# Turning the rows of experts 2 to 7 on VectorE, by way of memory, in a fused attention and mixture-of-experts kernel

## The chip, the cores and the metric

The kernel runs on one core of a Trainium2 chip. A core has a matrix engine (TensorE, PE in the profile, with its weight loads shown apart as PEld), a vector engine (VectorE, DVE), a scalar engine (ScalarE, ACT), a general engine (GpSimd, POOL) and a synchronization engine (SyncE, SP) that here only issues transfers. Transfers run on 16 DMA engines and are issued from the instruction streams of SP and POOL. Each engine works through its own stream in order, and waits where an instruction's operands are not ready. The metric is device time in microseconds (us), the median of several runs.

## The reference: what is computed

Sliding-window attention over 8 batches, 8 heads and 576 positions (half of the heads with a dilated window), and after it a top-1 mixture of 8 experts over the 4608 tokens of 512 features:

```
x = attn_out.transpose(0, 2, 1, 3).reshape(B * S, H * D)      # 4608 x 512
logits = x @ w_gate;  expert_idx = argmax(logits);  gate_w = softmax(logits)[expert_idx]
for e in range(8):
    xe = x[expert_idx == e]
    out[expert_idx == e] = gate_w * (relu(xe @ w1[e]) @ w2[e])   # w1 512x1024, w2 1024x512
```

## The kernel before

**Attention and routing.** The attention stage writes its rows to `x_d` in memory. Routing puts into the table `pair`, for every expert, the token number and the gate of each of its slots, in blocks of 128.

**Experts.** Each expert has a `Static` job of four blocks of 128 rows (512 slots; expert 0 has two blocks and two more as `rest0`). What does not fit goes to `Dynamic` jobs, called overflow below: five big ones (`DBIG`) of 128 rows, and two small ones (`Tail`) of 32 rows. Which expert an overflow job belongs to is known only at run time; `blocks_info` looks that up (seven indirect reads into `look`), and finds the rows `ti` and the weight rows `wi`.

**Weights.** An expert has 8 units of 512 KB, four of `w1` and four of `w2`. A unit is loaded into one of three `raw` buffers and split into a high and a low fp32r part (`split_unit`: ScalarE copies, VectorE subtracts, two halves each). A load is asked for three units ahead. Static units are loaded by SP; overflow units by POOL, with an indirect transfer that takes its 128 row numbers from `wi`.

**Rows.** A block's rows are gathered by POOL (`gather`, an indirect transfer into one of four `xg` buffers). A matrix multiplication needs them with features on the partitions, so TensorE turns them, four 128x128 transposes against `ident` into one PSUM tile `tpx` (only one buffer), ScalarE copies the high part out and VectorE subtracts for the low part (`prep`, `prep_x`; lines 799, 802, 806 for static blocks, 900, 902, 903 for big overflow jobs, 995 and 1002 for tails).

**Order.** In the expert stage the streams of TensorE, VectorE and ScalarE are in the order in which the program is written (`manual_schedule`); those of POOL and SP are ordered by the scheduler. While expert i runs (8 pieces of its first layer `hps`, f = 0 to 7, 12 matrix multiplications each; then 4 blocks of its second layer `yps` in halves, k = 0 to 7, 12 each), the 8 units of an overflow job and the 8 of expert i+1 are split, that overflow job runs in two layers of 24 (`hpd`, `ypd`) with its own transposes `tph`, and expert i+1's rows are gathered and turned. Each finished block is scaled by ScalarE into `y` and written out by POOL (`finish`).

Of the kernel before, what the change touches and what calls it, by code (L numbers as in the profile page):

```python
# [25 lines left out]
NE = 8  # L26
# [24 lines left out]
TAIL = 32  # L51
DBLK = DBIG + DTAIL
# [71 lines left out]
def _layout(q, k, v, wg, w1, w2):  # L124
# [8 lines left out]
    def spans(a, step, width):  # L133
# [17 lines left out]
            w1.reshape(NE, 4, P, DF),  # L151
# [4 lines left out]
    w = np.ascontiguousarray(w).reshape(NE * 8 * P, DF)  # L156
# [4 lines left out]
def attention_moe_kernel(ctx, tc, qk, v, wg, w, cst, tok, end, slots, mask, zero, out):  # L161
# [594 lines left out]

    def finish(y_ps, gate, it_col):
        y = pools["y"].tile([P, DM], F32, name="y")
        nc.scalar.activation(y, y_ps, AF.Copy, scale=gate)  # L759
        nc.gpsimd.indirect_dma_start(  # L760
            out=out,
            out_offset=bass.IndirectOffsetOnAxis(ap=it_col, axis=0),
            in_=y,
            in_offset=None,
        )

    class Static:
        def __init__(self, e, rows=N, nblk=4):
# [5 lines left out]
            self.ahead = {}  # L774

# [12 lines left out]
        def fetch(self, i):  # L788
            self.xg[i] = gather(self.it[i], self.rows)
# [20 lines left out]
        def prep(self, i):  # L810
            self.turn_x(i)
            self.high_x(i)
            self.low_x(i)
# [5 lines left out]
        def load(self, u):  # L819
            raw = raws.tile([P, DF], F32, name="raw")  # L820
            r = (self.e * 8 + u) * P
            nc.sync.dma_start(raw, w[r : r + P])
# [61 lines left out]
    class Dynamic:  # L884
        def __init__(self, ti=None, wi=None, gate=None, fixed=None, units=None):
            self.ti, self.wi, self.gate, self.fixed = ti, wi, gate, fixed
            self.units = [] if units is None else units
            self.ahead = {}

        def fetch_x(self):  # L890
# [4 lines left out]
            self.xg = gather(self.it)  # L895

        def prep_x(self):
            tp = pse.tile([P, 4, P], F32, tag="E", name="tpx")
# [8 lines left out]
        def load(self, u):  # L907
            raw = raws.tile([P, DF], F32, name="raw")
            nc.gpsimd.indirect_dma_start(  # L909
                out=raw,  # L910
                out_offset=None,
                in_=w,
                in_offset=bass.IndirectOffsetOnAxis(ap=self.wi[:, u : u + 1], axis=0),
            )
            return raw

# [58 lines left out]
    class Tail(Dynamic):  # L975
# [3 lines left out]
        def __init__(self, ti, gate, parts, wi, tag):  # L979
            super().__init__(ti, wi, gate)  # L980
            self.own, self.parts, self.tag = ti, parts, tag

        def fetch_x(self):
            self.xg = gp.tile([P, DM], F32, name="xg")
            nc.gpsimd.indirect_dma_start(
                out=self.xg[:TAIL],
                out_offset=None,
                in_=x_d[:],
                in_offset=bass.IndirectOffsetOnAxis(ap=self.own, axis=0),
            )  # L990

        def prep_x(self):
            tp = pse.tile([P, 4, TAIL], F32, tag="E", name="tpx")
            for c in range(4):
                nc.tensor.transpose(
                    tp[:, c], self.xg[:TAIL, c * P : (c + 1) * P], ident[:TAIL, :TAIL]
                )
# [4 lines left out]
            nc.scalar.copy(self.x, tp)  # L1002

        def unit(self, to, u):
            if u % 2 == 0 and to in (0, 1, 2):
                self.pair = new_unit(to)
            if to in (0, 1, 2):
                to = self.pair[:, u % 2].bitcast(F32)
            nc.gpsimd.indirect_dma_start(
                out=to,  # L1010
                out_offset=None,
                in_=w,
                in_offset=bass.IndirectOffsetOnAxis(ap=self.wi[:, u : u + 1], axis=0),
            )
# [182 lines left out]
    def blocks_info(d, nd):  # L1197
# [30 lines left out]
        at_ = dsp.tile([P, nd], I32, name=f"at{nd}")  # L1228
        nc.vector.tensor_tensor(at_, sl, cc[:, C_AT - C_ATT : C_AT + nd - C_ATT], op=ALU.add)
        yield  # L1230
        look = dsp.tile([P, nd, 2], I32, name=f"look{nd}")
        for i in range(nd):
            nc.gpsimd.indirect_dma_start(
# [3 lines left out]
                in_offset=bass.IndirectOffsetOnAxis(ap=at_[:, i : i + 1], axis=0),  # L1237
            )
            yield
        shp = [P, nd, NE]  # L1240
        wi = dsp.tile(shp, I32, name=f"wi{nd}")
        nc.vector.tensor_tensor(
            wi,
            ew.broadcast_to(shp),
            cc[:, C_PU - C_ATT : C_PU + NE - C_ATT].unsqueeze(1).broadcast_to(shp),
            op=ALU.add,
        )
        yield
        no = dsp.tile([P, nd], F32, name=f"no{nd}")
# [4 lines left out]
        ti = dsp.tile([P, nd], I32, name=f"ti{nd}")  # L1254
        nc.vector.tensor_tensor(ti, look[:, :, 0], no, op=ALU.add)
        yield
        info["blocks"] = ti, wi, look[:, :, 1].bitcast(F32)
# [3 lines left out]
    def make_list():  # L1261
# [84 lines left out]
        yield from blocks_info(d_all, DBLK)  # L1346
        dti, dwi, dgt = info["blocks"]
        parts = dsp.tile([P, DTAIL], I32, name="parts")
        nc.vector.tensor_scalar(
# [3 lines left out]

        dyn[:] = [Dynamic(dti[:, i : i + 1], dwi[:, i], dgt[:, i : i + 1]) for i in range(DBIG)]
        dyn[DBIG:] = [
            Tail(
                dti[:TAIL, DBIG + i : DBIG + i + 1],
                dgt[:, DBIG + i : DBIG + i + 1],
                parts[:, i : i + 1],
                dwi[:, DBIG + i],  # L1360
                tag,
            )
            for i, tag in enumerate(("xd", "hs"))
        ]
# [8 lines left out]
    with tc.manual_schedule(engines=ENGS):  # L1373
# [13 lines left out]

        nx.begin()
        r0.fetch_x()
        nx.fetch(0)  # L1390
        r1.fetch_x()
# [3 lines left out]
        st_.layer2(0, range(6))  # L1395
        some_gates(1)
        st_.layer2(1, range(6))
        r0.prep_x()
        nx.fetch(2)
        some_gates(1)  # L1400
        st_.layer2(0, range(6, 8))
        r0.layer1([0])
        some_gates(1)
        nx.prep(0)
        nx.fetch(3)
        part(0)
        some_gates(1)
        r0.layer1([1])
        some_gates(1)
        r0.turn([0])  # L1410
        r1.prep_x()
        r0.turn([1])
# [189 lines left out]
```

## Time and profile before

| what | value |
|---|---|
| median of 3 runs | 639.79 us (639.29 to 640.07) |
| profiled execution, its own time | 634.56 us |
| its span, first to last instruction | 632.8 us |
| TensorE busy | 604.8 us (96%) |
| VectorE, ScalarE, POOL busy | 348.5, 314.2, 249.7 us |
| granted TensorE clock, mean | 0.984 |
| moved by DMA | 138.70 MB, mean 219 GB/s |

The profiled execution is 5.2 us shorter than the median of the runs; of its own time 1.8 us lie around the span. Attention and routing take about the first 190 us of the span, experts the rest. A row of a timeline merges like instructions that follow each other; its first number is its start, so that the start of the next row less its own start is what it took of the engine's stream. A row of windows gives the stretch and its length, then busy time and number of instructions of PE, PEld, DVE, ACT and POOL, the granted clock (1.00 is 2.4 GHz), the DMA share and GB/s.

### The profile page before, as it was taken

The numbers are of one execution on the slowest core, as the hardware profiler recorded it, in microseconds if no ns is written. First come the engines' busy times: TensorE is split into PE (matmuls) and PEld (weight loads), VectorE is DVE, ScalarE is ACT, GpSimd is POOL, SyncE is SP. The second block draws the span as 40 slices with busy tenths as digits, with TensorE's granted clock in tenths as the row PEclk, the third lists the DMA queues.
The fourth block names the chain that finished last, engine by engine and source line by source line (L and its number), as shares of the span: only waits on it lengthen the run. The fifth ranks groups of instructions, "written<-read, shape, count | busy, mean of one in ns | idle before, by whom it ended". The sixth has DMA issues, their size and how long they took to land. (4 is left out here: it accounts for less than half of the span.)

```text
span 632.8 us, 13319 instructions
## 1 busy us (share of the span) xinstructions
PE 604.8 (96%) x5299; PEld 492.2 (78%) x5299; DVE 348.5 (55%) x749; ACT 314.2 (50%) x606; POOL 249.7 (39%) x301
## 2 busy tenths in 40 slices
PE   7999999998889999899999999999999999999992
PEld 6877887776677888788888888888888888887771
DVE  3777888889584559325554455455454544552100
ACT  2667677687523645334653455456445544552200
POOL 0332465689835540642133224222421244242221
PEclk7999999999899999999999999999999999999997
DMA  8999999976226575453675376547735765865310
GB/s 332 409 398 412 400 405 409 340 238 204 67 87 232 155 234 198 122 178 120 197 232 184 116 236 221 172 137 231 236 128 181 239 199 161 307 223 218 133 55 21
DMA packets 43295, 138.70 MB, mean 219 GB/s; under 512 B 8880, under 2 KB 10288, under 8 KB 43184
## 3 DMA queue, kind: packets, MB, share of 16 engines
q1 hardware_dynamic: 23376, 78.99, 35.6%
q0 software_dynamic: 19856, 58.84, 27.6%
q8 instruction: 42, 0.69, 0.4%
q14 instruction: 21, 0.17, 0.1%
HBM read 118.18 MB, written 21.63 MB: 221 GB/s over the span
## 5 line engine op out<-in xcount | busy, mean ns | idle before, releaser
L724 DVE TENSOR_TENSOR wu<-raw,wu 128x512 fp32r<-128x512 f32 x200 | 127.9, 687 | 85.6 <-ACT wu L723 85.6
L874 PE MATMUL yps<-wu,h 128*128 128x512 f32 x696 | 171.4, 398 | 0.0
L843 PE MATMUL hps<-x,wu 128*128 128x512 f32 (+1 forms) x720 | 165.2, 386 | 0.2 <-DVE h L855 0.2
L843 PEld LDWEIGHTS hps<-x,wu 128*128 128x128 f32 x720 | 132.0, 188 | 28.1 <-DVE h L855 0.4
L874 PEld LDWEIGHTS yps<-wu,h 128*128 128x128 f32 x696 | 128.1, 188 | 27.8 <-issue 0.8
L723 ACT CAST wu<-raw 128x512 fp32r<-128x512 f32 x200 | 112.1, 619 | 2.4 <-DMA raw<-in_w_dram 2.4
L854 ACT ACTIVATE h<-hps 128x512 fp32r<-128x512 f32 (+1 forms) x60 | 35.0, 583 | 97.0 <-PE hps L843 87.9
L855 DVE SCALAR_TENSOR_TENSOR h<-hps,h 128x512 fp32r<-128x512 f32 (+1 forms) x60 | 40.3, 672 | 77.4 <-ACT h L854 77.4
L909 POOL DMA_INDIRECT raw<-in_w_dram,wi x40 | 38.1, 952 | 96.8 <-DVE wu L724 92.6
L327 ACT COPY pts<-pt 96x512 f32<-96x512 f32 x72 | 41.9, 582 | 49.6 <-PE pt L322 48.7
L760 POOL DMA_INDIRECT out_dram<-y,pair x30 | 31.5, 1051 | 67.4 <-ACT y L759 38.8
L759 ACT ACTIVATE y<-yps,pair 128x512 f32<-128x512 f32 x28 | 19.3, 688 | 74.4 <-PE yps L874 47.9
L301 DVE TENSOR_REDUCE nm<-s 128x4 f32<-128x384 f32 x72 | 39.5, 549 | 23.8 <-PE s L290 23.7
L322 PE MATMUL pt<-ident,p 128*96 128x128 f32 x288 | 48.2, 292 | 2.5 <-ACT pts L327 2.3
L369 POOL DMA_DIRECT2D x_d<-xs x36 | 20.5, 569 | 67.4 <-DVE xs L357 30.8
L337 PE MATMUL o<-vr,pts 96*64 96x65 f32 x1152 | 43.9, 229 | 2.3 <-issue 1.4
L337 PEld LDWEIGHTS o<-vr,pts 96*64 96x64 f32 x1152 | 38.5, 142 | 9.6 <-issue 7.8
L749 POOL DMA_INDIRECT xg<-x_d,pair x30 | 30.7, 1025 | 35.8 <-PE tpx L799 18.4
L306 DVE TENSOR_TENSOR d<-s,nm 128x384 f32<-128x384 f32 x72 | 40.0, 557 | 4.6
L316 ACT ACTIVATE p<-d 128x384 f32<-128x384 f32 x72 | 37.5, 524 | 7.5 <-DVE d L306 7.4
L964 PE MATMUL ypd<-wu,hd 128*128 128x512 f32 x168 | 40.5, 392 | 0.0
L932 PE MATMUL hpd<-wu,xd 128*128 128x512 f32 x168 | 40.4, 395 | 0.0
(172 smaller groups left out, 694.8 us busy)
## 6 DMA issues: line engine op xcount, KB each, us to landing
raw<-in_w_dram SPq DMA_DIRECT2D x65, 512.0 KB, 4.3
qkr<-in_qk_dram SPq DMA_DIRECT2D x36, 576.0 KB, 8.7
vr<-in_v_dram SPq DMA_DIRECT2D x36, 520.0 KB, 8.4
x_d<-xs POOLq DMA_DIRECT2D x44, 128.0 KB
t_in<-tab SPq DMA_DIRECT2D x3, 320.0 KB, 4.1
x_d<-xs POOLq DMA_DIRECT2D x8, 112.0 KB
x_d<-xs POOLq DMA_DIRECT2D x8, 96.0 KB
tab<-in_zero_dram SPq DMA_DIRECT2D x2, 320.0 KB, 8.2
```

What stands on the lines that cost most here:

```text
L301: nc.vector.tensor_reduce(st["nm", n][:, g], st["s", n][g], axis=AX.X, op=ALU.max)
L306: nc.vector.tensor_tensor(st["d", n][:, g], st["s", n][g], st["nm", n][:, g].broadcast_to([P, HP, KB]), op=ALU.subtract,)
L322: nc.tensor.transpose(pt[:KB, h], st["p", n][:, g, h], ident)
L327: nc.scalar.copy(st["pts", n][:, g], st.pop(("pt", n))[:KB])
L337: nc.tensor.matmul(st["o", n][QB * j : QB * (j + 1), g, h], lhsT=pts[:, g, h, QB * j : QB * (j + 1)], rhs=vr[:KB, n % NRV, a : a + DH + 1] ...
L723: nc.scalar.copy(u[:, 0, sl], raw[:, sl])
L724: nc.vector.tensor_tensor(u[:, 1, sl], raw[:, sl], u[:, 0, sl].bitcast(F32), op=ALU.subtract)
L843: nc.tensor.matmul(hps[:, : self.ns], lhsT=u[:, wpart, fs], rhs=self.x[:, xpart, c, : self.ns], start=(k == 0), stop=(k == 11),)
L855: nc.vector.scalar_tensor_tensor(h[:, 1, :n], hps[:, :n], 0.0, h[:, 0, :n].bitcast(F32), op0=ALU.max, op1=ALU.subtract,)
L874: nc.tensor.matmul(yps, lhsT=self.h[f][:, hpart, ts], rhs=u[:, wpart, fs], start=f == 0 and k == 0, stop=f == 7 and k == 2,)
L932: nc.tensor.matmul(hps, lhsT=self.x[:, xpart, c], rhs=u[:, wpart, ns], start=(k == 0), stop=(k == 11),)
L964: nc.tensor.matmul(self.yps, lhsT=self.h[f // 4][:, hpart, f % 4], rhs=u[:, wpart, fs], start=f == 0 and k == 0, stop=f == 7 and k == 2,)
```

## The change

It does five things.

1. For experts 2 to 7 and all overflow jobs, the transposes on TensorE go. POOL gathers a block one expert ahead (`collect`); SP writes it to a buffer `rows` in memory (`put`); about an expert later SP reads it back with four transfers of 32 partitions (`quarters`, pieces of 512 bytes), so that feature group i of all 128 rows stands on partitions 32i to 32i+31; VectorE transposes the 16 blocks of 32x32 in place with one instruction, ScalarE copies the high part and VectorE subtracts (`turned_split`). The rows of `w1` are permuted on the host to fit; experts 0 and 1 keep the transposes on TensorE and have an unpermuted copy of `w1`.
2. Tails gather 128 pieces of 128 features and are turned by one VectorE instruction on 128x128.
3. Overflow weights are loaded by SP at an address that SP reads from `wi` (`value_load`), not by POOL.
4. The streams of POOL and SP too are now in written order.
5. The list of overflow blocks (`make_list`) is computed earlier, partly beside the end of expert 0; the seven look-ups are issued one at a time; the last part of it, `no`, `ti` and `parts`, comes later. The gate scatters of expert 0's stage are issued earlier, and `r0.layer2` stands in other pieces.

```diff
+    def put(xg):
+        rows = dram.tile([P, DM], F32, name=f"rows{len(kept)}")
+        kept.append(rows)
+        nc.sync.dma_start(rows[:], xg)
+        return rows
+    def quarters(rows):
+        xg = gp.tile([P, DM], F32, name="xg")
+        parts = rows[:].rearrange("(s t) (i c) -> i t s c", s=NQ, i=NQ)
+        for i in range(NQ):
+            nc.sync.dma_start(
+                xg[i * QD : (i + 1) * QD].rearrange("t (s c) -> t s c", s=NQ), parts[i]
+            )
+        return xg
+    def turned(xg, n=NQ):
+        blocks = xg.rearrange("p (s c t) -> p s c t", s=n, c=4)
+        nc.vector.transpose(blocks, blocks)
+        return blocks.rearrange("p s c t -> p c s t")
+    def turned_split(x, xg):
+        rows = turned(xg)
+        x = x.rearrange("p i c (s t) -> p i c s t", s=NQ)
+        nc.scalar.copy(x[:, 0], rows)
+        nc.vector.tensor_tensor(x[:, 1], rows, x[:, 0].bitcast(F32), op=ALU.subtract)
...
         def load(self, u):
             raw = raws.tile([P, DF], F32, name="raw")
-            nc.gpsimd.indirect_dma_start(
...
+            self.bring(raw, u)
             return raw
+        def bring(self, to, u):
+            if self.at is None:
+                self.at = nc.sync.value_load(self.wi, min_val=0, max_val=(NE - 1) * 8 * P)
+            nc.sync.dma_start(to, w[bass.ds(self.at + u * P, P)])
...
-    with tc.manual_schedule(engines=ENGS):
+    with tc.manual_schedule(engines=ENGS | {mybir.EngineType.Pool, mybir.EngineType.SP}):
...
             st_, nx, dy = statics[i], statics[i + 1], dyn[i - 2]
-            nx.fetch_x()
+            nx.begin()
             for f in range(8):
+                if f == 0:
+                    dy.fetch_x()
+                elif f in (2, 3, 4, 5):
+                    nx.fetch(f - 2)
                 st_.layer1([f])
-                if f in (1, 3, 5, 6):
+                if f in (0, 2, 4, 5):
                     split()
-                if f == 4:
+                if f == 3:
                     dy.prep_x()
+                if f == 6:
+                    nx.prep(0)
             for k in range(2):
                 dy.layer1([k])
                 split()
+            nx.prep(1)
             for k in range(8):
                 st_.layer2(k // 2, halves[k % 2])
...
-                if k in (0, 2, 4, 6):
-                    nx.prep(k // 2)
-                if k == 4 and i < NE - 2:
-                    dyn[i - 1].fetch_x()
+                if k in (2, 4):
+                    nx.prep(k // 2 + 1)
+                if k % 2 == 0 and i < NE - 2:
+                    statics[i + 2].collect(k // 2)
+                if k % 2 and i < NE - 2:
+                    statics[i + 2].put(k // 2)
+                if k == 5 and i < NE - 2:
+                    dyn[i - 1].collect()
+                if k == 7 and i < NE - 2:
+                    dyn[i - 1].put()
```

TensorE's stream around expert 2 stood before as follows (`hps` is the first layer, `tpx` turned rows, `hpd` and `tph` the overflow job, `yps` the second layer):

```order
L843 MATMUL hps<-x,wu 128x512 x60
L900 MATMUL tpx<-ident,xg 128x128 x4
L843 MATMUL hps<-x,wu 128x512 x36
L932 MATMUL hpd<-wu,xd 128x512 x24
L874 MATMUL yps<-wu,h 128x512 x12
L949 MATMUL tph<-ident,hs 128x128 x4
L799 MATMUL tpx<-ident,xg 128x128 x4
L874 MATMUL yps<-wu,h 128x512 x12
```

The same stretch of TensorE's stream now, with the line numbers of the changed kernel:

```order
L895 MATMUL hps<-x,wu 128x512 x96
L995 MATMUL hpd<-wu,xd 128x512 x24
L926 MATMUL yps<-wu,h 128x512 x12
L1012 MATMUL tph<-ident,hs 128x128 x4
L926 MATMUL yps<-wu,h 128x512 x12
L1027 MATMUL ypd<-wu,hd 128x512 x12
```

The `tpx` rows are gone; nothing else in it moved.

SP's stream from the end of expert 0 to the end of the kernel stood before as follows (`raw` is a weight unit, `left` the count for a loop at the end that runs no time here):

```order
L822 DMA raw<-in_w_dram 128x1024 x7
L1556 TENSOR_LOAD left
L1556 ISA x2
L822 DMA raw<-in_w_dram 128x1024 x44
L1560 COMPARE_AND_BRANCH
```

At the boundary between two experts SP's stream now reads as follows (`rows` is the buffer in memory; the two writes are the next expert's last block and the overflow job's rows, each read is four quarters):

```order
L978 DMA raw<-in_w_dram 128x1024
L764 DMA rows_5449<-xg 128x512
L764 DMA rows_5451<-xg 128x512
L772 DMA xg<-rows_5451 32x4x128 x4
L978 ISA
L978 DMA raw<-in_w_dram 128x1024
L772 DMA xg<-rows_5272 32x4x128 x4
```

Weight loads, which stood alone in SP's stream, now stand behind writes that wait for gathers and reads that wait for writes.

VectorE's stream in the second layer of expert 1 stood before as follows (`no`, `ti`, `parts` are the end of the look-up, `x` the low part of the turned rows of expert 2):

```order
L724 TENSOR_TENSOR wu<-raw,wu 128x512 x2
L1250 SCALAR_TENSOR_TENSOR no_4272<-look_4224,cc 128x7
L1255 TENSOR_TENSOR ti_4274<-look_4224,no_4272 128x7
L1349 TENSOR_SCALAR parts<-ti_4274,cc 128x2
L724 TENSOR_TENSOR wu<-raw,wu 128x512 x4
L806 TENSOR_TENSOR x<-tpx,x 128x4x128 x4
```

VectorE's stream at the same place now:

```order
L1303 SCALAR_TENSOR_TENSOR no_4271<-look_4073,cc 128x7
L727 TENSOR_TENSOR wu<-raw,wu 128x512 x2
L782 STREAM_TRANSPOSE xg<-xg 128x512
L790 TENSOR_TENSOR x<-xg,x 128x4x128
L727 TENSOR_TENSOR wu<-raw,wu 128x512 x2
L782 STREAM_TRANSPOSE xg<-xg 128x512
L790 TENSOR_TENSOR x<-xg,x 128x4x128
```

Each block has one more VectorE instruction, and `no`, which waits for the look-ups, stands at the end of the first layer of expert 1.

## Rows read from the trace of the kernel before

**Rows 1.** The page: busy us of each engine, share of the span, instructions.

```profile
PE 604.8 (96%) x5299; PEld 492.2 (78%) x5299; DVE 348.5 (55%) x749; ACT 314.2 (50%) x606; POOL 249.7 (39%) x301
```

**Rows 2.** Windows of the stages of experts 1, 2, 6 and 7.

```profile
227.54:275.71 48.17, 46.35 (x211) 37.77 (x210) 28.50 (x68) 21.35 (x39) 19.84 (x20) 1.00 0.62 198
275.71:334.20 58.49, 58.49 (x270) 47.88 (x268) 28.76 (x45) 28.81 (x52) 16.14 (x16) 1.00 0.51 164
...
509.30:567.12 57.82, 57.82 (x269) 47.78 (x268) 30.06 (x47) 29.91 (x54) 23.53 (x24) 1.00 0.70 228
567.12:621.20 54.08, 54.06 (x397) 41.73 (x395) 7.53 (x12) 10.22 (x20) 14.80 (x16) 1.00 0.37 132
```

**Rows 3.** The tile tpx: its instructions, ns min/median/max, starts.

```profile
L799 PE MATMUL tpx<-ident,xg x120: 270/272/476, 156.2 to 564.3; 128*128 128x128 f32 x120
...
L900 PE MATMUL tpx<-ident,xg x28: 271/272/273, 198.2 to 523.2; 128*128 128x128 f32 x28
...
L995 PE MATMUL tpx<-ident,xg x8: 220/222/243, 575.4 to 583.5; 32*128 32x32 f32 x8
```

**Rows 4.** Timeline of TensorE, second layer of expert 1.

```profile
260.76 0.60 PE L799 MATMUL tpx<-ident,xg 128*128 128x128 f32 x4
261.11 3.04 PE L874 MATMUL yps<-wu,h 128*128 128x512 f32 x12
265.97 0.66 PE L799 MATMUL tpx<-ident,xg 128*128 128x128 f32 x4 [1.82 <-DVE x L806]
266.38 3.03 PE L874 MATMUL yps<-wu,h 128*128 128x512 f32 x12
```

**Rows 5.** Timeline of TensorE, second layer of expert 2.

```profile
304.14 2.90 PE L874 MATMUL yps<-wu,h 128*128 128x512 f32 x12
306.87 0.60 PE L949 MATMUL tph<-ident,hs 128*128 128x128 f32 x4
307.31 0.60 PE L799 MATMUL tpx<-ident,xg 128*128 128x128 f32 x4
307.66 3.02 PE L874 MATMUL yps<-wu,h 128*128 128x512 f32 x12
310.52 2.89 PE L964 MATMUL ypd<-wu,hd 128*128 128x512 f32 x12
...
322.37 2.88 PE L874 MATMUL yps<-wu,h 128*128 128x512 f32 x12
325.09 0.60 PE L799 MATMUL tpx<-ident,xg 128*128 128x128 f32 x4
```

**Rows 6.** Timeline of TensorE, first layer of expert 7, a tail's transposes.

```profile
575.38 0.43 PE L995 MATMUL tpx<-ident,xg 32*128 32x32 f32 x4
575.73 5.73 PE L843 MATMUL hps<-x,wu 128*128 128x512 f32 x24
```

**Rows 7.** Timeline of VectorE, second layer of expert 1.

```profile
262.28 0.17 DVE L1250 SCALAR_TENSOR_TENSOR no<-look,cc 128x7 f32<-128x7 int32 x1 [4.31 <-DMA look<-pairs,at]
```

**Rows 8.** Groups by line: busy us, mean ns, idle before and releaser.

```profile
L724 DVE TENSOR_TENSOR wu<-raw,wu 128x512 fp32r<-128x512 f32 x200 | 127.9, 687 | 85.6 <-ACT wu L723 85.6
...
L760 POOL DMA_INDIRECT out_dram<-y,pair x30 | 31.5, 1051 | 67.4 <-ACT y L759 38.8 <-ACT wu L723 15.3 <-ACT xt L1035 5.8
...
L749 POOL DMA_INDIRECT xg<-x_d,pair x30 | 30.7, 1025 | 35.8 <-PE tpx L799 18.4 <-DVE pair L441 7.1 <-issue 6.9
...
L759 ACT ACTIVATE y<-yps,pair 128x512 f32<-128x512 f32 x28 | 19.3, 688 | 74.4 <-PE yps L874 47.9 <-issue 19.6 <-PEq L1560 7.0
```

**Rows 9.** Issues of SP's loads, ns min/median/max, and their landing.

```profile
L822 SPq DMA_DIRECT2D raw<-in_w_dram x65: 327/328/493, 71.0 to 559.3; - x65
...
DMA to landing us min/median/max: 3.4/4.3/10.3
```

**Rows 10.** DMA issues: KB each, median us to landing.

```profile
out_dram<-in_zero_dram SPq DMA_DIRECT2D x1, 256.0 KB, 8.8
...
ident<-in_cst_dram SPq DMA_DIRECT2D x1, 64.0 KB, 5.2
```

More of the change, by code (lines that the diff above doesn't have):

```diff
@@ L788, in fetch, with collect, put @@
         def fetch(self, i):
-            self.xg[i] = gather(self.it[i], self.rows)
+            if self.e < ROWS:
+                self.xg[i] = gather(self.it[i], self.rows)
+            else:
+                self.xg[i] = quarters(self.rows_[i])
+        def collect(self, i):
+            if self.e >= ROWS:
+                self.rows_[i] = gather(pair[:, self.e * BPE + i, 0:1])
+        def put(self, i):
+            if self.e >= ROWS:
+                self.rows_[i] = put(self.rows_[i])
         def fetch_x(self):
@@ L985, in fetch_x @@
             nc.gpsimd.indirect_dma_start(
-                out=self.xg[:TAIL],
+                out=self.xg[:, :P],
                 out_offset=None,
-                in_=x_d[:],
-                in_offset=bass.IndirectOffsetOnAxis(ap=self.own, axis=0),
+                in_=x_d[:].rearrange("n (i d) -> (n i) d", i=NQ),
+                in_offset=bass.IndirectOffsetOnAxis(ap=self.parts, axis=0),
             )
         def prep_x(self):
[L993 to L997, printed above, removed]
             box = pools["d"].tile([P, DF], F32, tag=self.tag, name="xt")
@@ L1345, in make_list, with ready @@
         info.update(first=first_, step=step_, cum=cum, big=nbig, left=left)
[L1346 to L1347 removed]
         parts = dsp.tile([P, DTAIL], I32, name="parts")
+        def ready(dti, dwi, dgt):
+            dyn[:] = [
+                Dynamic(dti[:, i : i + 1], dwi[:, i : i + 1], dgt[:, i : i + 1], turned=True)
+                for i in range(DBIG)
+            ]
+            dyn[DBIG:] = [
+                Tail(
+                    dgt[:, DBIG + i : DBIG + i + 1],
+                    parts[:, i : i + 1],
+                    dwi[:, DBIG + i : DBIG + i + 1],
+                    tag,
+                )
+                for i, tag in enumerate(("xd", "hs"))
+            ]
+        yield from blocks_info(d_all, DBLK, ready)
+        dti = info["blocks"][0]
         nc.vector.tensor_scalar(
@@ L1386, in some_gates, with some @@
                 gates_later.pop(0)()
+        after = statics[2]
+        items = make_list()
+        def some(n):
+            for _ in range(n):
+                next(items, None)
         nx.begin()
         r0.fetch_x()
+        r1.fetch_x()
+        some_gates(2)
         nx.fetch(0)
-        r1.fetch_x()
+        some_gates(2)
         nx.fetch(1)
@@ L1417, in attention_moe_kernel @@
         nx.prep(1)
-        some_gates(1)
+        some(4)
         r1.layer1([0])
-        some_gates(1)
         nx.prep(2)
         part(2)
-        some_gates(1)
-        all_gates()
+        some(4)
         r1.layer1([1])
+        some(4)
+        r0.layer2(range(4, 6))
         r1.turn([0])
         nx.prep(3)
+        r0.layer2(range(6, 8))
+        some(4)
+        for n in range(2):
+            after.collect(n)
         r1.turn([1])
         part(3)
-        r0.layer2(range(4, 8))
+        for n in range(2):
+            after.put(n)
         part(4)
         r1.layer2()
+        for n in range(2, 4):
+            after.collect(n)
     jobs = [(lambda: statics[1], 0, u) for u in range(5, 8)]
@@ L1466, in tails_load @@
             job.unit(grp, u)
-    with tc.manual_schedule(engines=ENGS):
+    with tc.manual_schedule(engines=ENGS | {mybir.EngineType.Pool, mybir.EngineType.SP}):
         st_, nx = statics[1], statics[2]
-        items = make_list()
-        def some(n):
-            for _ in range(n):
-                next(items, None)
-        nx.fetch_x()
+        nx.begin()
         for f in range(8):
@@ L1565, in attention_moe_kernel @@
         ti, wi, gate = info["blocks"]
-        job = Dynamic(ti, wi[:, 0], gate)
+        job = Dynamic(ti, wi, gate, turned=True)
+        job.collect()
+        job.put()
         job.fetch_x()
```

139 lines of the change are left out of this document (73 added, 66 removed).

## The prediction

> **What bounds the kernel now.** I read the windows by stage first, because a share over the whole span mixes attention and experts. From expert 2 on TensorE is busy for the whole of each window, 58.49 of 58.49 us in expert 2 and 57.82 of 57.82 in expert 6, at granted clock 1.00, while VectorE has about half (28.76 and 30.06) and the DMA share is 0.51 and 0.70 [rows 2]. Only expert 1 has a hole, 48.17 us with 46.35 busy. Over the span the order is the same [rows 1]. So in the expert stage a microsecond that leaves TensorE's stream leaves the time, and one given to VectorE, ScalarE, POOL or SP costs nothing until TensorE waits for it. I then read TensorE's timeline for what the transposes take, and VectorE's for the hole.
>
> **What is removed.** The tile tpx has 120, 28 and 8 instructions on TensorE [rows 3], four to a block, so 30 static blocks, 7 overflow blocks and 2 tails. Two blocks of expert 0, four of expert 1 and two of `rest0` keep theirs, so 24 + 5 + 2 = 31 groups of four go. A record lasts 272 ns, but records overlap, and the price is from start to start: 307.31 to 307.66 is 0.35 us for four [rows 5], 260.76 to 261.11 the same [rows 4], and a tail's from 575.38 to 575.73 too [rows 6]. 31 x 0.35 = 10.9 us.
>
> The Trainium skill weighs this differently: "TensorE: Matmul & The Clock Gate", section "Part 4: PE-mode transpose", gives about 275 ns for one 128x128 transpose in a kernel. The records agree with it, at 272 ns, but the spacing of the starts does not. By the page 116 transposes would be worth an estimated 31.9 us and the sum below would be some 23 us larger.
>
> What follows a transpose is slower too. Twelve multiplications behind a `tpx` run from 307.66 to 310.52, 2.86 us; twelve behind others take 2.73 (304.14 to 306.87) and 2.72 (322.37 to 325.09) [rows 5]. If all of that 0.13 comes back 31 times, it is 4.0 us; if the pace has another cause, nothing. In experts 2 to 6 one block in four has the job's own `tph` right ahead of the `tpx`, and that stays. I take half, 2.0 us.
>
> The hole: in expert 1 the third transpose group waits 1.82 us for VectorE [rows 4], since there is one `tpx` buffer, and VectorE stood 4.31 us at `no` for the look-ups [rows 7]. In the new order `no` stands behind the first layer, some 10 us after the last look-up is asked for, and nothing of expert 2 passes through `tpx`. 1.8 us go.
>
> **What is added.** VectorE gets one transpose of 128x512 a block, five an expert. No row shows one. The nearest is its subtraction on the same shape, 0.687 us [rows 8]; nothing at the low end, and 1.4 us, twice that row, at the high one. I take 0.69, since the elements are as many. That is 3.4 us on 30 of 58 (7.0 at 1.4), and VectorE stays under two thirds. ScalarE's copy and the subtraction stay, with SBUF as source; a weight's subtraction already reads SBUF, in those 0.687 us. Its cover is the first layer: a block waits at f = 3 or 6, and TensorE goes on as long as it has a free `hps` buffer of three, about two pieces of 2.8 us.
>
> SP gets per expert 5 writes, 20 quarters and 8 overflow loads, at 0.328 us an issue [rows 9] 10.8 us more of about 58; POOL loses 8 loads at about a microsecond. Memory gets 5 x 2 x 0.26 MB = 2.6 MB an expert, 45 GB/s more on 164 to 228 [rows 2]; at the ratio of rate to share there (228 at 0.70) that is 0.14 more share, 0.65 to 0.84. The weight loads still fit. SP also reads `wi` once a job; no row shows such a read, and I bound it by nothing and 2 us. I book none of this, and price the cover that hides it next.
>
> **Which wait is new.** At an expert boundary SP waits for a gather (write of block 3), then for its own write (overflow rows), and a weight load stands behind. I count from T, the end of the last second-layer piece. The gather of block 3 stands in POOL's stream behind the output write of block 2 and the overflow gather, from one block (5.6 us) before T: 0.69 for `y`, 1.05, 1.03 and 1.03 on POOL [rows 8], 0.9 between them, and about 2.2 to land, 6.9 in all, T + 1.3. SP gets there only behind the load that waits for the split at k = 7, which follows `y` of block 3: 0.69 + two halves of 0.687 and a copy, T + 2.7. So the gather is there. The two writes then land in something between a weight unit's shortest 3.4 [rows 9] and 8.8 us (a row of the busy start) [rows 10]; I take 4.3, the median of a twice larger load: T + 7.3. The quarters are issued by T + 8.6 and land 3.4 to 5.2 us later [rows 9, 10]. `prep_x` of the overflow job comes at f = 3, T + 4 x 2.8 + 1.3 = T + 12.5. That is about even; late by 3 us it delays VectorE and ScalarE but not TensorE, whose next need of the job is at T + 22. The weight load behind the quarters is issued at T + 9, lands 4.3 later, and is split at f = 5, after T + 16.8: 3.5 us of cover. With the writes at 8.8 us it would be short by 1.
>
> On this place "DMA: Bandwidth & Descriptors" of the Trainium skill, section "Bandwidth", speaks against the change: transfers under 64 KB are dominated by their descriptors, and each quarter is 64 KB. The row agrees so far as 64 KB took 5.2 us where 512 KB took 4.3; by it a quarter would be no quicker than a unit. [...]
>
> **End of expert 0.** The gate scatters now alternate with gathers. POOL's sums then end earlier, and `y` of `rest0` no longer holds ScalarE. Between the second half of r1's transposed rows and their use I find about a microsecond of cover, so I book nothing, and 0 to 2 us of loss for the range. Of the list of overflow blocks some two dozen small VectorE instructions, and one small multiplication, move ahead into this stretch; the stretch that they leave has 28.5 us of VectorE in 48 [rows 2], and I book nothing for them either.
>
> **Sum.** 10.9 + 2.0 + 1.8 = 14.7 us, 12.7 to 16.7 by its bounds. Of the profiled execution's 634.56 that leaves 619.9; the median shown is 5.2 higher, and I subtract from it: 639.8 - 14.7 = 625.1 us. Attention keeps its order on every engine.
>
> **Rivals.**
> *The relay is late (slower).* SP is stuck behind a write or a quarter, the weights behind it come late, and TensorE waits in each of experts 2 to 7. For it: the boundary's weight cover is 3.5 us and the writes' landing is known only within 3.4 to 8.8. Against it: three units are loaded ahead, and the second layer's puts come behind splits that are later than their gathers. It decides from 14.7 / 6 = 2.5 us an expert; at 4 us it is 639.8 - 14.7 + 24 = 649. Chance 0.13.
> *Part of the gain.* The transposes go, but the slow start behind them was not theirs, and VectorE's chain transpose, copy, subtract, in order, or the tight place at the end of expert 0, gives back 1 us an expert: 639.8 - 12.7 + 6 = 633; 628 to 637. Chance 0.20.
> *It does nothing: transfers set the pace.* Then TensorE would wait for weights in the freed slots. Against it: share 0.51 to 0.70 now, and only VectorE is waited for. 639.8, chance 0.05.
> *The whole record counts.* Each transpose blocks TensorE for 0.272 us: 116 x 0.272 + 1.8 = 33.4, 606 us. The starts at 0.35 for four speak against it; the row decides. Chance 0.02. "TensorE: Matmul & The Clock Gate" of the Trainium skill gives that length too.
>
> **Numbers.** The forecast has 0.60, its own range is 622 to 628. With the partial case the range holds 0.8: 621 to 635. A measurement of this kernel tells about 0.2%, 1.3 us, from no change. Faster: 0.60 + 0.20 + 0.02 = 0.82; same 0.05; slower 0.13.
>
> **What the changed profile would show.** Right: no `tpx` row from expert 1's first layer on, TensorE busy without a hole from expert 1 on, expert windows of about 56 us, twelve multiplications nearer to 2.73 us throughout, a VectorE transpose of 0.5 to 0.9 us, loads from SP landing in 4 to 6 us. Wrong: waits of TensorE for `wu` or `x`, at f = 0 to 5 or in an overflow job's layers; SP's queue waiting on writes of `rows` for more than 5 us a time; multiplications that keep 2.86 us; or a clock under 1.00 in the expert stage.

## The result and the profile after

The changed kernel took 632.86 us (628.39 to 634.06, four runs) where the kernel before took 639.86 (639.29 to 640.07) in the same series of runs, on one chip (an expectation below calls it a session): ratio 0.9873, interval 0.9846 to 0.9901, 7.0 us faster. In two other series it took 621.78 for 633.43 (0.9811, 0.9784 to 0.9837) and 621.90 for 633.38 (0.9807, 0.9775 to 0.9840), 11.6 and 11.5 us faster. So there are two numbers to explain: the 11.6 us, and what the first series takes back of them. The forecast was 625.1 us.

The page of the changed kernel, busy time of each engine, answers to [rows 1]:

```profile
PE 596.9 (95%) x5175; PEld 484.7 (77%) x5175; DVE 364.2 (58%) x786; ACT 315.5 (50%) x606; POOL 196.3 (31%) x245
```

TensorE has 7.9 us less and 124 instructions less, VectorE 15.7 us more, POOL 53 us less. Where that becomes time is seen by stage. The windows of the changed kernel: end of expert 0, expert 1, experts 2 and 6, and expert 7 up to TensorE's last multiplication (columns as in [rows 2]):

```profile
194.23:237.67 43.44, 40.07 (x189) 32.32 (x187) 24.93 (x59) 18.06 (x34) 24.92 (x24) 0.96 0.51 167
237.67:281.83 44.16, 44.16 (x193) 36.06 (x192) 25.79 (x53) 21.41 (x38) 18.33 (x18) 1.00 0.85 264
281.83:338.03 56.20, 56.20 (x250) 45.85 (x248) 32.15 (x50) 29.29 (x52) 7.17 (x7) 1.00 0.73 221
...
506.37:561.94 55.57, 55.57 (x249) 45.85 (x248) 33.04 (x52) 29.72 (x54) 9.03 (x9) 1.00 0.74 236
561.94:615.04 53.10, 53.10 (x389) 41.15 (x387) 7.96 (x14) 10.34 (x20) 6.74 (x7) 1.00 0.44 169
```

Expert 2 went from 58.49 to 56.20 us and expert 1 from 48.17, with a hole, to 44.16 without one [rows 2]. From expert 1 on TensorE never stands. The first line is the odd one: 43.44 us with 3.37 idle and the granted clock at 0.96.

The transposes behind it. The tile `tpx` on TensorE in the changed kernel, count and ns min/median/max, where [rows 3] had 120, 28 and 8:

```profile
L846 PE MATMUL tpx<-ident,xg x24: 270/273/476, 158.4 to 230.2; 128*128 128x128 f32 x24
...
L963 PE MATMUL tpx<-ident,xg x8: 270/272/273, 203.2 to 211.8; 128*128 128x128 f32 x8
```

And the instruction on VectorE that does their work now:

```profile
L782 DVE STREAM_TRANSPOSE xg<-xg x31: 300/704/712, 262.1 to 577.0; 128x512 f32<-128x512 f32 x29, 128x128 f32<-128x128 f32 x2
```

124 transposes are gone and 31 instructions of VectorE have come, 704 ns each for a whole block.

What the stages don't show is the end. Here are both kernels on the chip of the second series, the kernel before first and then the changed one, in three windows: end of expert 0, expert 1 to TensorE's last multiplication, and from there to the end of the span (us, TensorE's busy time, granted clock, DMA share, GB/s):

```profile
187.07:225.18 38.11, 38.10 (x186) 1.00 0.61 199
225.18:618.68 393.50, 391.81 (x1947) 1.00 0.56 184
618.68:630.30 11.62, 0.00 (x0) 0.72 0.06 23
```

```profile
187.94:226.23 38.29, 38.29 (x188) 1.00 0.58 189
226.23:604.13 377.90, 377.63 (x1821) 1.00 0.72 231
604.13:619.20 15.07, 0.00 (x1) 0.66 0.06 20
```

The experts give 15.6 us. The end, in which TensorE does nothing, takes 3.45 back. Attention and the end of expert 0 differ by 1.0. That makes 11.1 for these two executions, 11.6 for the medians.

### The profile page after: what moved, and what is told of

It is laid out like the page before. It is cut to its first block, busy times and chain, and to the rows that moved or that the text cites. A ratio compares the mean times of both kernels' runs of the same rounds, so it can differ in the third digit from the quotient of the medians.

```text
span 630.1 us, 13462 instructions
## 1 busy us (share of the span) xinstructions
PE 596.9 (95%) x5175; PEld 484.7 (77%) x5175; DVE 364.2 (58%) x786; ACT 315.5 (50%) x606; POOL 196.3 (31%) x245
## 5 line engine op out<-in xcount | busy, mean ns | idle before, releaser
L926 PE MATMUL yps<-wu,h 128*128 128x512 f32 x696 | 166.4, 394 | 0.0
L895 PE MATMUL hps<-x,wu 128*128 128x512 f32 (+1 forms) x720 | 163.3, 385 | 0.2 <-DVE h L907 0.2
L926 PEld LDWEIGHTS yps<-wu,h 128*128 128x128 f32 x696 | 129.4, 188 | 29.1 <-issue 0.8
L795 POOL DMA_INDIRECT out_dram<-y,pair x30 | 29.7, 990 | 193.8 <-ACT y L794 127.5
L752 POOL DMA_INDIRECT xg<-x_d,pair x30 | 31.9, 1062 | 102.2 <-DVE x L790 55.7
L340 PE MATMUL o<-vr,pts 96*64 96x65 f32 x1152 | 45.4, 232 | 2.1 <-issue 1.9
L995 PE MATMUL hpd<-wu,xd 128*128 128x512 f32 x168 | 41.7, 403 | 0.0
L325 PEld LDWEIGHTS pt<-ident,p 128*96 128x96 f32 x288 | 29.6, 131 | 11.9 <-ACT pts L330 4.8
```

The costliest lines, as they stand in the source:

```text
L325: nc.tensor.transpose(pt[:KB, h], st["p", n][:, g, h], ident)
L340: nc.tensor.matmul(st["o", n][QB * j : QB * (j + 1), g, h], lhsT=pts[:, g, h, QB * j : QB * (j + 1)], rhs=vr[:KB, n % NRV, a : a + DH + 1] ...
L895: nc.tensor.matmul(hps[:, : self.ns], lhsT=u[:, wpart, fs], rhs=self.x[:, xpart, c, : self.ns], start=(k == 0), stop=(k == 11),)
L926: nc.tensor.matmul(yps, lhsT=self.h[f][:, hpart, ts], rhs=u[:, wpart, fs], start=f == 0 and k == 0, stop=f == 7 and k == 2,)
L995: nc.tensor.matmul(hps, lhsT=self.x[:, xpart, c], rhs=u[:, wpart, ns], start=(k == 0), stop=(k == 11),)
```

## The experiments

Theory at the start: the expert stage gives what the sum said, and the end of expert 0, in its new order, takes part of it back. Rival: the loss there belongs to that execution or chip.

**Both kernels again, unaltered** (no edit).

> The changed kernel once more, unaltered, to see which of its losses come back. Theory (the loss lies in the program): the wait of 3.37 us for the third transpose group of expert 1, with ScalarE's 3.69 us ahead of the output of expert 0's second block, comes back, and the stage from the last attention piece to expert 1's first layer takes 45 us again; the time is 632 to 634. Rival (the loss is a stall of that one execution): ScalarE goes on at once there, the stage takes 40 to 42 us, and the profiled execution comes out at 628 or below.

> The kernel before once more, unaltered. Its first profiled execution took 634.56 us where its others took 639.3 to 640.1. Theory (attention loses a few us to stretches at half the clock, whose number differs from one execution to the next): attention ends at another place than 187.9 us of the span, by 2 to 5 us, and the expert stage keeps its 393.6 us within 1 us. Rival: attention ends at 187.9 again and the 5 us lie in the expert stage.

Measured: the changed kernel 621.78 us, before 633.48 beside 633.43 of the other runs in its series (ratio 1.0008, 0.9982 to 1.0033). In this series the rival held: the stop of the first profile is not there. It came again later, in the series of spare_gathers. In the first profile TensorE's timeline reads (a bracket gives the idle time before a row and what the profile says ended it):

```profile
212.31 1.62 PE L926 MATMUL yps<-wu,h 128*128 128x512 f32 x6
...
216.50 0.60 PE L846 MATMUL tpx<-ident,xg 128*128 128x128 f32 x4
216.85 3.04 PE L995 MATMUL hpd<-wu,xd 128*128 128x512 f32 x12
223.25 1.12 PE L846 MATMUL tpx<-ident,xg 128*128 128x128 f32 x4 [3.37 <-DVE x L853]
```

and ScalarE's, a little earlier:

```profile
214.94 0.59 ACT L1016 CAST hd<-tph 128x512 fp32r<-128x512 f32 x1 [0.85 <-PE yps L926]
219.22 0.69 ACT L794 ACTIVATE y<-yps,first_g 128x512 f32<-128x512 f32 x1 [3.69 <-remote]
```

The piece of `yps` at 212.31 is the last that this `y` reads, so by these records ScalarE had its data from 213.9 on. It was free from 215.53 and stood until 219.22. Behind it stood the split of a weight, behind that the low part of `x` that frees the `tpx` buffer, and so TensorE. What followed, in windows of TensorE:

```profile
219.00:223.20 4.20, 0.89 (x4) 1.00 0.35 115
223.20:227.00 3.80, 3.75 (x12) 0.55 0.58 225
```

Behind the idle stretch the granted clock is at the lower of its two levels, 1.2 GHz, for most of the next window. In the second series the same instructions follow one another without a gap:

```profile
210.21 0.60 PE L846 MATMUL tpx<-ident,xg 128*128 128x128 f32 x4
210.56 3.03 PE L995 MATMUL hpd<-wu,xd 128*128 128x512 f32 x12
213.43 0.60 PE L846 MATMUL tpx<-ident,xg 128*128 128x128 f32 x4
```

And the same `y` there:

```profile
207.68 0.69 ACT L794 ACTIVATE y<-yps,first_g 128x512 f32<-128x512 f32 x1 [0.67 <-PE yps L926]
```

So this `y` waits for TensorE's `yps`. The trace also keeps the steps of the semaphore by which TensorE tells of it, which no view prints. In the second series the step stands at 207.66, where the records end that piece. In the first it stands at 219.20, 5.3 us behind the recorded end, and that is what `<-remote` means here: a step with no instruction's end beside it. So it was TensorE's signal that came late, and ScalarE followed it. The profile models the ends of multiplications, so it doesn't show whether the work itself ended late, nor why.

The kernel before had 393.50 us in its expert stage against 393.63 in its first profile, and attention ended at 187.07 by this window's edge instead of 189.44, 2.4 us earlier, so its theory held (the 187.9 that it names is not this edge). That first profile, 634.56 us, lies near this series's 633.43 and not near the 639.3 to 640.1 of the runs it was shown with.

**Expert 0's end in its old order.**

```diff
-        some_gates(2)
         nx.fetch(0)
-        some_gates(2)
         nx.fetch(1)
...
-        all_gates()
+        some_gates(1)
         r0.layer2(range(4))
...
         part(2)
+        some_gates(1)
+        all_gates()
...
-        r0.layer2(range(4, 6))
         r1.turn([0])
...
-        r0.layer2(range(6, 8))
...
+        r0.layer2(range(4, 8))
```

> The changed kernel with the gate scatters, the reading of the gates and the overflow's second-layer pieces of expert 0's end where the kernel before has them; the list of overflow blocks stays early and POOL and SP stay in written order. Theory (the new order of expert 0's end costs the 5.3 us seen there): the stage takes 40 to 41 us and the time falls by 4 to 5 us, to 628. Rival (the order is not the cause): the stage keeps 44 to 45 us or both kernels have it at 40 to 42, and the time is within 1 us of the changed kernel's.

Measured: 622.60 us beside 621.78 of the changed kernel in this series, the stage 38.25 us beside 38.29. The new order costs nothing that shows in this series. The stop of the first series didn't come here with either order, so this run doesn't say whether the order plays a part in it.

**Transposes back on TensorE, the rest of the change kept.**

```diff
# prep, for static blocks
-                turned_split(self.x[:, :, :, i * P : (i + 1) * P], self.xg[i])
+            self.turn_x(i)
+            self.high_x(i)
+            self.low_x(i)
...
# prep_x, for overflow blocks
-                turned_split(self.x, self.xg)
```

> The changed kernel with its relay through memory, its loads and its order, but the transposes of the static and overflow blocks of experts 2 to 7 back on TensorE and through PSUM (the rows then stand in another order than the weights, so this part of the computation is changed). Theory (each group of four costs 0.35 us and its follower 0.07 to 0.13): 29 groups, 12 to 14 us slower than the changed kernel, expert windows of 58.4 us. Rival (the gain came from the other edits, the loads by SP and the order): windows stay at 56.2 to 57 us, under 5 us slower. Second rival (TensorE now waits itself for the quarters): windows above 60 us, more than 20 us slower.

Measured: 644.75 us, 23.0 above the changed kernel; the expert stage took 397.75 us, 19.9 more than 377.90, with windows of 58.4 to 60.7. That is more than the first theory said, and for the second rival's reason in small. A row of TensorE's waits (us in all, times, longest):

```profile
PE tpx L956 <- DMA xg<-rows: 6.2, 4, 1.8
```

With the overflow block's transposes on TensorE, TensorE itself waits for the quarters, 1.8 us at worst. In the changed kernel VectorE waits there and TensorE doesn't: `DVE xg L782 <- DMA xg<-rows` has 9.1 us in four waits, the longest 3.4, and TensorE waits once from expert 1 on, for 0.3 us.

**A group of transposes priced alone.**

```diff
+    def idle_turns():
+        tp = pse.tile([P, 4, P], F32, tag="E", name="tpi")
+        for c in range(4):
+            nc.tensor.transpose(tp[:, c], ident, ident)
```

It stands ahead of each of the 29 calls of `turned_split`.

> The changed kernel with one extra group of four transposes of the identity on TensorE ahead of each of the 29 blocks that VectorE now turns; nothing reads them and nothing of the computation changes. It prices a group alone. Theory (0.35 us for the group and 0.07 to 0.15 us for the multiplications behind it): 12 to 14.5 us slower than the changed kernel of the same chip, expert windows 58.3 to 58.7, the twelve multiplications behind a group at 2.86 to 2.88 us. Rival (the group alone, the follower's pace has another cause): 10.2 us. Second rival (a group blocks TensorE for its whole record, 4 x 0.272 us): 31 us.

Measured: 634.21 us beside 621.90, 12.3 more. The expert stage, and a group in the timeline of this kernel:

```profile
227.41:618.12 390.71, 390.70 (x1937) 1.00 0.69 224
```

```profile
293.33 0.60 PE L795 MATMUL tpi<-ident 128*128 128x128 f32 x4
293.68 3.04 PE L901 MATMUL hps<-x,wu 128*128 128x512 f32 x12
296.56 3.66 PE L1002 MATMUL hpd<-wu,xd 128*128 128x512 f32 x15
```

390.71 less the 377.82 of the changed kernel in this series is 12.9 us for 29 groups, 0.44 each: 0.35 from start to start (293.33 to 293.68) and 0.09 behind it. Twelve multiplications behind this group take 2.88 us, as behind `tpx` before [rows 5], though these transposes read nothing that anyone waits for. So the slow start belongs to the group. By the length of the records, 0.272 us each, it would have been 31.6 us. "TensorE: Matmul & The Clock Gate" of the Trainium skill, section "Part 4: PE-mode transpose", gives about 275 ns for one 128x128 transpose (of bf16) in a kernel, as long as these records (of f32); the measurement decides for 0.44 us a group of four.

**The end: the loop behind the experts.** The loop for further overflow blocks runs no time here, but its transfers moved from POOL to SP with the change.

```diff
# loop_pool, on the changed kernel
-        job = Dynamic(ti, wi, gate, turned=True)
-        job.collect(); job.put()
+        job = Late(ti, wi[:, 0], gate)        # gather, transposes on TensorE, weights by POOL
# before_loop_sp, on the kernel before
-        job = Dynamic(ti, wi[:, 0], gate)
+        job = Late(ti, wi[0:1, 0, 0:1], gate) # the eight weights by SP
```

> The changed kernel with only the loop behind the last expert (run once for each further overflow block) as the kernel before has it: rows gathered and weights loaded by POOL, transposes on TensorE. Theory (the 3.5 us that the changed kernel loses between TensorE's last multiplication and the end of the span come from this loop's eight loads, write and quarters on SP): the distance from TensorE's end to the span's end falls from 15.1 to 11.6 us and the time by 3.5 us against the changed kernel of the same chip; expert windows stay at 56.2. Rival (the end waits for writes that now land later, whatever the loop holds): the distance stays at 15 us, and the time within 1 us.

> The kernel before with one part of the change alone: in the same loop the eight weight loads go to SP. Theory (SP's part in the loop costs at its end even when the loop is not entered): 2.5 to 3.5 us slower than before, distance from TensorE's end to the span's end 14 to 15 us instead of 11.6. Rival (it is the relay of the rows in the loop, or nothing of the loop): within 1 us of before.

Measured: 624.39 us, 2.5 above the changed kernel, and 632.41, a ratio of 0.9986 (0.9961 to 1.0010) to before. The end took 17.19 us in the first and 10.00 in the second: the opposite of the theory, which fell. In these profiles the eight loads on SP in the loop make the end 1.6 us shorter (before_loop_sp; the whole time shows no change clear of noise), and with the relay of the rows it is 2.5 us (loop_pool).

The rows of the last source line, by engine, then showed what takes the time (count, ns min/median/max). Before, then the changed kernel:

```profile
L1598 POOLq DRAIN  x3: 51/103/4154, 627.8 to 632.5; - x3
```

```profile
L1689 POOLq DRAIN  x3: 45/103/8324, 621.0 to 629.9; - x3
```

All engines meet at the end, and they wait for the longest of POOL's three drains there. It is the first of the three, at 621.0 in the changed kernel; the expectations below call it POOL's last drain. It takes 8.32 us instead of 4.15, and the step `INC_SWDGE_SEM` on POOL ahead of it 2.21 instead of 1.18:

```profile
L1560 POOLq INC_SWDGE_SEM  x1: 1181/1181/1181, 625.2 to 625.2; - x1
```

```profile
L1649 POOLq INC_SWDGE_SEM  x1: 2214/2214/2214, 617.1 to 617.1; - x1
```

Together they take 5.2 us more. Less the 1.6 to 2.5 that SP in the loop saves, that is 2.7 to 3.6, and the end grew by 3.0 to 3.45 in the profiles. "VectorE: DVE Perf Modes" of the Trainium skill, section "The DRAIN you can't avoid", says that the drains which come with every kernel's start and end take about 12 ns on all engines. At the end of the changed kernel those of the other engines agree, with 7 to 17 ns; POOL's long one takes 892 to 8977 ns in the kernels here, and the measurement decides.

**The changed kernel a third time**, beside these:

> The changed kernel a third time, unaltered, beside the others of this group. Its two sessions gave 0.987 and 0.981 of before. Theory (the expert stage gives 15.6 us, the end takes 3.5, and what is left differs with stalls and the clock in attention from one execution to the next): 11 to 12.5 us faster than before in median, single executions between 5 and 14; windows 56.2 and end 15.1 in the profile. Rival (the first session's 7 us is the rule): 6 to 8 us faster.

Measured: 621.90 us, 11.5 faster than before, single runs 618.62 to 624.47. Expert stage 377.82, end 14.66, end of expert 0 38.75.

**Which part lengthens the drain.** Weight loads put back on POOL for the tails alone, for the five blocks alone, and taken from POOL in the kernel before:

```diff
# tails_pool (for blocks_pool: range(DBIG))
+            info["wrows"] = rows                      # a table of weight rows, 128 x 56
+            for i in range(DBIG, DBLK):
+                dyn[i].wrows = info["wrows"][:, i]    # bring() then gathers on POOL
# before_sp_loads, in load() and unit() of the kernel before
-            nc.gpsimd.indirect_dma_start(out=..., in_=w, in_offset=...)
+            nc.sync.dma_start(to, w[bass.ds(self.at + u * P, P)])
```

> The loop theory fell: with the loop as before the end grew. What grows is POOL's last drain, 8.32 us in every kernel with the change and 4.15 in every kernel without it, and the step ahead of it, 2.21 for 1.18. This kernel is the changed one with only the 16 weight loads of the two tails, the last loads of the program, back on POOL (rows of weights gathered, as before). Theory A (the drain depends on what POOL issued late): drain 4.15 again, the end 4 to 5 us shorter, time 4 to 5 us below the changed kernel's, about 617.5 where it takes 621.9. Theory B (it depends on how many transfers POOL issued over the whole program, or on the five blocks' 40 loads): drain 8.32, time within 1 us of the changed kernel's. Theory C (it depends on what the engine's program holds at its end, the relay or the tail's gather): drain 8.32 too.

> The changed kernel with the 40 weight loads of the five overflow blocks back on POOL, as rows gathered, and the tails' 16 left on SP. Theory B (number of POOL's transfers): drain 4.15 to 6 us and the end shorter by 2 to 4 us; against that POOL's gathers and output writes stand behind its loads, which wait for free buffers, so TensorE may wait at an expert's boundary: 1 to 6 us an expert. Theory A or C: drain 8.32 and nothing gained. In all of them the time is not below the changed kernel's by more than 3 us.

> The kernel before with one part of the change alone: the weight loads of the overflow blocks, the tails and the loop go to SP. Theory A or B (the drain depends on POOL's loads): drain 8.32, end 14 to 15 us, 3 to 4.5 us slower than before as far as the end goes; if SP's loads come earlier than POOL's did, nothing is won, since TensorE did not wait for weights. Theory C: drain 4.15, time within 1 us of before's, or 1.6 us less as with the loop alone on SP.

Measured: before_sp_loads 637.12 us, ratio 1.0046 (1.0027 to 1.0064): this part of the change alone costs 3.0 us. Its end and its drain:

```profile
619.62:634.00 14.38, 0.00 (x0) 0.68 0.05 18
```

```profile
L1595 POOLq DRAIN  x3: 51/103/8319, 624.9 to 633.7; - x3
```

The end is 2.8 us longer than the 11.62 of before. tails_pool 610.79 us, ratio 0.9633 (0.9609 to 0.9657): the best kernel here, 23.3 us below before. Its windows (end of expert 0, experts, end) and its drain:

```profile
185.69:224.29 38.60, 38.23 (x188) 1.00 0.59 188
224.29:599.79 375.50, 374.27 (x1821) 1.00 0.73 232
599.79:607.70 7.91, 0.00 (x0) 0.66 0.11 41
```

```profile
L1711 POOLq DRAIN  x3: 45/103/892, 606.0 to 607.5; - x3
```

The end fell by 6.8 to 7.2 us, more than theory A said, since the drain is below the one of before. But the drain of blocks_pool takes 2852 ns, which A doesn't give. The time of blocks_pool is 636.08 us, ratio 1.0017 (0.9996 to 1.0038), for another reason. A row each of POOL's, VectorE's and TensorE's waits (us in all, times, longest):

```profile
POOL raw L979 <- DVE wu L727: 95.0, 20, 12.1
```

```profile
DVE xg L782 <- DMA xg<-rows: 30.3, 4, 8.8
```

```profile
PE hps L895 <- DVE h L907: 14.3, 4, 4.8
```

With the blocks' loads on POOL the gathers stand behind loads that wait for free buffers, up to 12.1 us for one. The relay is late by up to 8.8 us for VectorE, and TensorE waits up to 4.8 us at a time for what VectorE does behind that.

The drains against the number of POOL's transfers, counted from the list of DMA issues:

| kernel | transfers by POOL | weight loads among them | long drain at the end, ns |
|---|---|---|---|
| changed, loop_pool, before_sp_loads | 222 | 0 | 8324, 8324, 8319 |
| tails_pool | 238 | 16 | 892 |
| blocks_pool | 262 | 40 | 2852 |
| before, before_loop_sp | 278 | 56 | 4154 |

None of the theories A to C gives these drains. From 238 to 262 and from 262 to 278 each transfer adds 0.082 and 0.081 us. If this slope holds at 222 too, the count there has to be one that began earlier.

**Spare transfers.**

```diff
+            if f > 3:            # expert 7
+                spare_gather()   # 128 pieces of 512 B, read by nothing
+                spare_gather()
```

> The changed kernel, its weight loads left on SP, with two additions that change nothing of the result: the table of weight rows of tails_pool, computed and not used (it takes 224 bytes a partition and moves every tile behind it), and eight spare gathers of 128 pieces on POOL during expert 7, which nothing reads. They bring POOL's transfers from 222 to 230. Theory, drain: POOL's last drain was 0.89, 2.85 and 4.15 us with 238, 262 and 278 transfers, 0.0815 us more for each, which points to a count that starts again behind transfer 227 and had not yet done so at 222 (8.32 us). With 230 it then takes 0.2 to 0.3 us and the end 6 to 8 us instead of 14.7. Rival: the drain depends on which loads POOL issues (weights), and stays at 8.32. Theory, pace: the two kernels with the table have expert windows of 43.5 and 55.4 us instead of 44.2 and 56.2 because tiles stand elsewhere, so this one has them too. Rival: the pace came from the loads on POOL; windows stay at 44.2 and 56.2. With both theories the time is 610 to 613, as tails_pool; with neither 621 to 623.

Measured: 627.62 us, in a series where before took 639.85, ratio 0.9797 (0.9768 to 0.9826). The drain:

```profile
L1722 POOLq DRAIN  x3: 45/103/8977, 615.7 to 625.2; - x3
```

The theory of the drain fell as it was put: 230 transfers don't shorten it, they add 0.65 us, 0.082 for each of the eight. The slope is the same, the restart isn't at 227. All the transfers that these kernels add have 128 pieces, so a price for each transfer isn't told apart from one for each piece. The windows of experts 1, 2 and 3 of this kernel:

```profile
236.23:279.75 43.52, 43.52 (x194) 36.04 (x193) 25.90 (x54) 21.29 (x38) 18.14 (x18) 1.00 0.83 260
279.75:335.13 55.38, 55.38 (x249) 45.82 (x248) 31.97 (x50) 28.97 (x52) 6.99 (x8) 1.00 0.70 230
335.13:390.53 55.40, 55.40 (x250) 45.83 (x249) 33.08 (x52) 29.82 (x54) 10.93 (x11) 1.00 0.78 251
```

The theory of the pace held against its rival: with the table and without loads on POOL TensorE needs 0.6 to 0.8 us less an expert for the same multiplications.

## Why the prediction was right, and where it was not

The range of 621 to 635 us holds the 632.86 of the first series. The forecast of 625.1, with its own range of 622 to 628, does not: there 7.0 us came of the 14.7. It lies in the wider range by the partial case. In the two series in which before takes 633.4, 11.5 and 11.6 us came, and the terms below add up to them within some tenths.

*What bounds the kernel, and what is removed*: right. TensorE's stream set the expert stage, and what left it left the time. 10.9 us for 31 groups at 0.35 stands. (The estimate by the whole record's length has a slip: 31.9 us in place of the 10.2 of the same 29 groups makes the sum some 22 us larger, not 23.)

*What follows a transpose*: right in kind, too small. I took half of 4.0 us. idle_turns gives 0.09 us a group on 29 groups; on all 31 that is 2.8.

*The hole*: right, expert 1 has none. 10.9 + 2.8 + 1.8 = 15.5 us, and the expert stage gave 393.50 - 377.90 = 15.6.

*What is added*: VectorE's transpose took 0.704 us where I took 0.69, the DMA share is 0.73 to 0.77 in experts 2 and 3 and 0.74 in expert 6 where I worked out 0.65 to 0.84. These were worth nothing, as said.

*Which wait is new*: right, and tight. In the second series the writes land in 4.3 us in median (2.3 to 6.3) and the quarters in 3.6 (1.9 to 7.2), sooner than the 4.6 of a weight unit, where I let a quarter be no quicker. The quarters of the overflow block were "about even": late by up to 3.4 us for VectorE, which its cover hid. pe_turn and blocks_pool show what stands behind that cover. The second is a late relay as in the first rival, though behind POOL's stream and not SP's, and it ate the whole gain.

*The step that failed* is in "What is added": SP gets the overflow loads, "POOL loses 8 loads at about a microsecond", and "I book none of this". I looked for the price of that move at the expert boundaries, where it costs nothing, and let the sum end at TensorE's last multiplication. before_sp_loads shows the price at the end of the program: 3.0 us, a drain of 8.32 us instead of 4.15. The sum should have read 15.5, less the 3.0 to 3.45 by which the end grew, less some tenths at the end of expert 0, about 12, and 11.5 and 11.6 were measured in two series.

*The end of expert 0*: the order that I priced at 0 to 2 us of loss costs 0.2 to 0.6 us (38.29 and 38.75 for 38.11). In the first profile the stage took 43.44. That is 5.2 us, and 11.6 less 5.2 would be 6.4, near the 7.0 of that series. This sum is argued, not shown: no profile shows the kernel before in an execution of 639.9, so what it loses there isn't known. Shown is that ScalarE's stop comes in both series of that kind, the first and that of spare_gathers, at the same `y` and at one `pts` of attention, and in no profile of the three series in which before takes 633 to 634. In both it follows a late signal of TensorE; why that is late is not known.

Of the rivals the partial case came nearest in its number, 633 for 632.86, and this is luck. It charged 6 us to VectorE's chain or to the tight place at the end of expert 0, and gave nothing back for the slow start. VectorE's chain took nothing, the slow start was worth 2.8 us, and the end, which it doesn't name, took 3 us. The end of expert 0 did take 5.2 us in the first profile, but behind a stop that is missing in both other series of the same program.

**Open.** Whether the drain falls somewhere between 231 and 238 transfers or only where POOL loads weights: the runs don't separate these, and that there is a count which begins again is itself read from the slope alone. The shorter pace with the table: its place in SBUF and its one instruction on VectorE came together. Of tails_pool's 11 us below the changed kernel (as ratios to before, in different series) the end explains 7 and the pace 2.3. The rest lies ahead of expert 0's end, where the stretches at the lower clock differ from profile to profile; TensorE gets there at 185.69 us of the span, and at 187.94 and 189.47 in the changed kernel.

## What to carry to other kernels

Make the sum against the whole span: read what stands after the last multiplication and ask which edit changes what an engine has to finish there. Price a suspected cost by adding it again where nothing depends on it; the idle transposes gave in one run what two theories argued over. Compare two kernels within one series only, and look for a stop at the same instruction in a second profile before building a story on it.

## What was not expected of the hardware

The first of POOL's three drains at the end took 0.9 to 9.0 us in these kernels, and the end waits for it. It grew by about 0.08 us with each transfer that POOL issued more (222 to 230, and 238 to 262 to 278), and it was far shorter at 238, with weight loads among them, than at 230 without. A table of 224 bytes a partition, computed and unused, went with windows of 55.4 instead of 56.2 us. In two of five series TensorE's signal for one piece came some 5 us behind its recorded end, ScalarE stood up to 3.7 us for it, and TensorE's granted clock fell behind the hole that this made.
